# A fused attention, feed-forward and expert kernel: SBUF tiles on the right side moved to multiples of 256 bytes, two operands offset by 32 and 64 bytes

## The chip, the core and the metric

The kernel runs on one core of a Trainium2 chip. Its time is the device time of one execution in microseconds; lower is better. The kernel before takes 744.92 us, the median of three runs (744.52, 744.92 and 745.54).

## What is computed

Three layers follow each other, all in fp32, for 4 sequences of 576 tokens (2304 in all) and a width of 512:

```python
# 1. attention of 8 heads of width 64; heads 0-3 see the last 32 positions, heads 4-7 every fourth of the last 128
attn = softmax(where(mask, q @ k.T / 8, -1e9)) ; x = attn @ v              # -> x [2304, 512]
# 2. feed-forward, squared relu
h = x @ w_in                                  # [512, 2048]
g = s * relu(h) ** 2 + b ; y = g @ w_out      # [2048, 512]
# 3. one of 8 experts per token, chosen by argmax of cosine similarity to an embedding
e = argmax(norm(y) @ norm(emb).T / tau)
out = gate * (relu(y @ w1[e]) @ w2[e])        # 512 -> 1024 -> 512
```

## The kernel before, in words

**Precision.** Each large product is made of three matmuls in the type fp32r: both operands are split into a high and a low part (`xhi`/`xlo`, `wih`/`wil`, `gh`/`gl`, `woh`/`wol`, and for the experts `xh`/`xl`, `wh`/`wl`, `hh`/`hl`), and `mm3` (lines 454 to 458) adds high times high, high times low and low times high into one PSUM bank. Every one of these matmuls has its own weight load: TensorE streams the moving operand of one matmul (`rhs`) while it loads the weights (`lhsT`) of the next, both from SBUF.

**Feed-forward stage** (`main`, `gemm1_mm`, `gemm2`). The tokens are in five groups; groups 0, 2, 3 and 4 have 512 tokens and group 1 has 256. A group takes 16 steps, one per 128 columns of the hidden layer. In each step the first product (`gemm1_mm`) makes 12 matmuls with `wih`/`wil` as weights and x as the moving operand, of 512 columns, or of 256 for group 1. The second product (`gemm2`), two steps later, has `gh`/`gl` as weights and `woh`/`wol` as moving operand, always of 512 columns: 12 matmuls, or 6 for group 1. Hence the first product has 64 steps of 12 matmuls of 512 columns and 16 steps of 12 of 256 columns; the second has 64 steps of 12 and 16 of 6. The attention of the next group, in small matmuls, is put between the steps. ScalarE and VectorE turn the raw weights into high and low parts during the first 22 steps (`Conversion`); after that the weights are resident.

**Where the tiles lie.** SBUF is allocated from both ends. Tiles in pools of the left side start, in the built program, at multiples of 256 bytes wherever a large matmul reads them: `xhi1`/`xlo1` (x of groups 1, 2 and 4, by the table `XH`), `wih`/`wil` of steps 11 to 15, `woh`/`wol` of steps 9 to 15, `gh`/`gl`, and for the experts the weights of odd units (`wp1`) and `hh`/`hl`. Tiles of the right side are laid down below a first tile `edge` (line 632, 8 floats, 32 bytes), and start 192 bytes past a multiple of 256: `xhi0`/`xlo0` (x of groups 0 and 3), `wih`/`wil` of steps 0 to 10, `woh`/`wol` of steps 0 to 8, and the weights of the experts' even units (`wp0`). The experts' x (`xp`, line 1081) lies below small tables and starts 128 bytes past a multiple of 256. Every slice of 128 columns inside these tiles is 512 bytes further, so a whole tile keeps its remainder.

**Expert stage** (`experts`). Tokens are gathered by expert into slots of 128 tokens, and 12 units, each with one expert's weights, always run. A unit serves a pair of slots or a single slot; unit 0 serves two pairs. In a pair, `g1_pair` makes 96 matmuls of 256 columns with the experts' weights as weights and `xh`/`xl` as the moving operand. In a single slot, `g1` has it the other way round: 24 matmuls with `xh`/`xl` as weights and the experts' weights, 512 columns, as moving operand. The second product `g2` makes 24 matmuls of 512 columns per tile, with `hh`/`hl` as weights and the experts' second weights as moving operand. Unit 0 has its weights on the right side and does two pairs; the six units with odd numbers have theirs on the left side and do a pair each; the five even ones behind unit 0 have theirs on the right side and do a single each.

**Order.** TensorE, and in most of the kernel ScalarE and VectorE, run in the order that the program was written in (`manual_schedule`). The change moves no instruction: on all five engines the order is the same, row by row, and so are the waits.

Of the kernel before, what the change touches and what calls it, by code (L numbers as in the profile page):

```python
# [7 lines left out]
F32 = mybir.dt.float32  # L8
F32R = mybir.dt.float32r
# [22 lines left out]
P = 128  # L32
# [4 lines left out]
UT = 256  # L37
NU = NT // UT
G = 512
GU = (2, 1, 2, 2, 2)  # L40
XH = (0, 1, 1, 0, 1)
NG = len(GU)
U0 = [sum(GU[:g]) for g in range(NG + 1)]
GT = [2 * n for n in GU]
T0 = [2 * n for n in U0]
NTE = T0[NG - 1]
SEGS = [(0, 0, 8), (1, 0, 16), (0, 8, 16)] + [(g, 0, 16) for g in range(2, NG)]
ORDER = [(g, f) for g, f0, f1 in SEGS for f in range(f0, f1)]
# [60 lines left out]
class Kern:  # L109
# [176 lines left out]
    def attn_x(self, cs):  # L286
        c, k = cs[0], len(cs)
        un, pr = c["un"], c["pr"]
        g = next(g for g in range(NG) if un < U0[g + 1])
        d0 = UT * (un - U0[g])  # L290
        hi, lo = (x[XH[g]][:, pr:pr + k, d0:d0 + UT] for x in (self.xhi, self.xlo))
        src = c["po"][:, :k * UT].rearrange("c (u t) -> c u t", u=k)
        if c["dil"]:
            src = src.rearrange("c u (j p) -> c u p j", j=4)
            hi, lo = (x.rearrange("c u (p j) -> c u p j", j=4) for x in (hi, lo))
        return hi, lo, src
# [86 lines left out]
    def attn_steps(self, n0, n1, ps):  # L383
# [4 lines left out]
        for n in range(n0, n1, 2):  # L388
            g = next(g for g in range(NG) if n // 4 < U0[g + 1])
            start, period, turn = TEMPO[g - 1]  # L390
# [68 lines left out]

    def gemm1_mm(self, g, fc, kcs=range(4)):  # L460
        n = P * GT[g]
        xh, xl = (x[XH[g]][:, :, :n] for x in (self.xhi, self.xlo))
        if 0 in kcs:
            self.ph = self.psf(f"ph{g}_{fc}")[:, :n]
        for kc in kcs:
            self.mm3(self.ph, self.wih[fc][:, kc], self.wil[fc][:, kc], xh[:, kc], xl[:, kc], kc == 0, kc == 3)
# [55 lines left out]
    def y_norm(self, g):  # L522
        if g < NG - 1:
            self.bg += self.logits_dve(g)
            return
        self.late_ssq = self.lpool.tile([P, 4], F32, tag="ssq", name=f"ssq{g}", bufs=2)
        for i in range(GT[g]):
            junk = self.mpool.tile([P, DM], BF16, tag="gh", name=f"junk{g}_{i}")
            self.nc.scalar.activation(junk, self.ysb[T0[g] + i], AF.Square, accum_out=self.late_ssq[:, i:i + 1])
# [98 lines left out]
    def run(self):  # L628
        tc, nc = self.tc, self.nc
        with tc.tile_pool(name="al", bufs=1, side="right") as al, tc.tile_pool(name="c", bufs=1) as c, \  # L630
                tc.tile_pool(name="dr", bufs=1, space=DRAM) as dr:
            al.tile([P, 8], F32, name="edge")
            self.lpool = c
            self.ydram = dr.tile([NT, DM], F32, name="ydram")
            first, late = ExitStack(), ExitStack()
            right = dict(bufs=1, side="right")
            with tc.tile_pool(name="wl", bufs=1) as wl:
                wr = first.enter_context(tc.tile_pool(name="wr", **right))
                self.weights_setup(wl, wr)
                ac = first.enter_context(tc.tile_pool(name="ac", **right))  # L640
                self.apool = first.enter_context(tc.tile_pool(name="ap", bufs=2, side="right"))
                self.mask = {}
                self.first_masks(ac)
                self.consts(c)
                self.mask_pool = ac

                def late_pools():
                    for nm in ("wp0", "rawp", "rpool", "xp"):
                        setattr(self, nm, late.enter_context(tc.tile_pool(name=nm, reuse_waits="tile", **right)))
                    self.psT = late.enter_context(tc.tile_pool(name="psT", space=PSUM, reuse_waits="tile", **right))  # L650
                self.phase1(wl, first, late, late_pools)
            kw = dict(bufs=1, reuse_waits="tile")
            with tc.tile_pool(name="wp1", **kw) as self.wp1, tc.tile_pool(name="hp", **kw) as self.hp, \
                    tc.tile_pool(name="pad", **kw) as self.pad, tc.tile_pool(name="psE", space=PSUM, **kw) as self.psE:
                self.experts()
            late.close()
# [421 lines left out]
    def xt(self, js, xs):  # L1078

        nc, w = self.nc, P * len(js)  # L1080
        xh = self.xp.tile([P, 4, w], F32R, tag="xh", name=f"xh{js[0]}")
        xl = self.xp.tile([P, 4, w], F32R, tag="xl", name=f"xl{js[0]}")
        for n, (j, x) in enumerate(zip(js, xs)):
            if n and j >= NEARLY:
                px = self.psE.tile([P, 512], F32, tag="h", name=f"px{j}", bufs=3)
            else:
                px = self.bank(f"px{j}", n == 0 and j >= 2)
            for i in range(4):
                nc.tensor.transpose(px[:, P * i:P * i + P], x[:, P * i:P * i + P], self.ident)
            p3 = px.rearrange("p (k t) -> p k t", k=4)  # L1090
            h, l = (y[:, :, P * n:P * n + P] for y in (xh, xl))
            nc.scalar.copy(h, p3)
            self.last_xl = nc.vector.tensor_sub(l, p3, h.bitcast(F32))
        return xh, xl
# [91 lines left out]
    def experts(self):  # L1186
# [63 lines left out]
        with tc.issue_after(self.last_gidx.ins):  # L1250
            self.gates_late()
        self.g2(2, 0, *hts, w[0])
        xt(1)
        behind.append((self.last_xl,))
        for a in range(2):
# [25 lines left out]
        with tc.manual_schedule(engines={mybir.EngineType.Activation, mybir.EngineType.DVE}):  # L1281
            for u in range(1, nstat, 2):
                more = u + 1 < nstat
                hts, part = self.g1_pair(runs[u], *xts.pop(u), w[u])
                h = hook({0: (u, 7), 1: (u, 8), 2: (u + 1, 1), 4: (u + 1, 2), 5: (u + 1, 3), 7: (u + 1, 4)})
                for i in range(4):
                    part(i, h)
                    if more and i == 0:
                        gather(u + 2)
                if more:  # L1290
                    xt(u + 1)
                self.g2(runs[u][0], 0, *hts, w[u], hook({2: (u + 1, 5), 6: (u + 1, 6)}))
                if more:
                    hs = self.g1(runs[u + 1][0], *xts.pop(u + 1), w[u + 1], hook({0: (u + 1, 7), 1: (u + 1, 8)}))
                self.g2(runs[u][1], 1, *hts, w[u], hook({2: (u + 2, 1), 6: (u + 2, 2)}))
                if more:
                    if u + 3 < nstat:
                        gather(u + 3)
                    hts = self.ht(runs[u + 1][0], hs)
                    xt(u + 2)  # L1300
                    self.g2(runs[u + 1][0], 0, *hts, w[u + 1],
                            hook({1: (u + 2, 3), 3: (u + 2, 4), 5: (u + 2, 5), 7: (u + 2, 6)}))
# [68 lines left out]
```

## Time and profile before

| | |
|---|---|
| median of three runs | 744.92 us |
| the profiled execution's own time | 742.73 us |
| its span, first to last instruction | 740.9 us |
| TensorE busy (matmuls) | 725.5 us, 98% of the span |
| VectorE busy | 532.8 us, 72% |
| ScalarE busy | 381.9 us, 52% |
| granted TensorE clock, mean | 0.998 of full speed |

Matmuls are pipelined: one shows as busy for longer than it holds the engine, so the busy time says only that TensorE is hardly ever without work. What a matmul costs is the distance from its start to the start of the next one, which the timeline gives. The shares of ScalarE and VectorE are averages over stages that differ, and a table by stretch is needed to see where one of them is close to full.

### The profile page before, as it was taken

The numbers are of one execution on the slowest core, as the hardware profiler recorded it, in microseconds if no ns is written. First come the engines' busy times: TensorE is split into PE (matmuls) and PEld (weight loads), VectorE is DVE, ScalarE is ACT, GpSimd is POOL, SyncE is SP. The second block draws the span as 40 slices with busy tenths as digits, with TensorE's granted clock in tenths as the row PEclk, the third lists the DMA queues.
The fourth block names the chain that finished last, engine by engine and source line by source line (L and its number), as shares of the span: only waits on it lengthen the run. The fifth ranks groups of instructions, "written<-read, shape, count | busy, mean of one in ns | idle before, by whom it ended". The sixth has DMA issues, their size and how long they took to land. (4 is left out here: it accounts for less than half of the span.)

```text
span 740.9 us, 13198 instructions
## 1 busy us (share of the span) xinstructions
PE 725.5 (98%) x4769; PEld 605.1 (82%) x4769; DVE 532.8 (72%) x1236; ACT 381.9 (52%) x831; POOL 61.6 (8%) x94
## 2 busy tenths in 40 slices
PE   9899999999999999999999999999999999999996
PEld 6677897787888888888888878788888888989894
DVE  6899998765776645877836779369668686868661
ACT  6899665765634424444424226425146565656550
POOL 6000000000000000000000000204213131311011
PEclk9999999999999999999999999999999999999999
DMA  9656653422311101111001006304263077878600
GB/s 278 201 186 212 189 169 127 148 70 74 93 52 58 52 23 43 51 52 58 23 1 58 0 1 227 114 1 132 83 197 103 30 231 261 297 257 285 224 30 26
DMA packets 34039, 87.34 MB, mean 118 GB/s; under 512 B 4326, under 2 KB 4326, under 8 KB 33840
## 3 DMA queue, kind: packets, MB, share of 16 engines
q1 hardware_dynamic: 30608, 76.22, 31.7%
q0 software_dynamic: 3360, 10.23, 4.2%
q8 instruction: 39, 0.64, 0.4%
q14 instruction: 32, 0.26, 0.1%
HBM read 92.72 MB, written 10.22 MB: 139 GB/s over the span
## 5 line engine op out<-in xcount | busy, mean ns | idle before, releaser
L1068 DVE TENSOR_TENSOR wl<-raw,wh 128x1024 fp32r<-128x1024 f32 x96 | 113.7, 1220 | 29.7 <-ACT wh L1067 29.7
L456 PE MATMUL ph<-xhi,wih 128*128 128x512 f32 (+1 forms) x320 | 119.6, 374 | 1.1 <-ACT wih L103 1.1
L458 PE MATMUL ph<-xhi,wil 128*128 128x512 f32 (+1 forms) x320 | 118.6, 371 | 0.9 <-DVE wil L106 0.8
L457 PE MATMUL ph<-xlo,wih 128*128 128x512 f32 (+1 forms) x320 | 118.5, 370 | 0.4 <-DVE xlo L304 0.4
L456 PE MATMUL py<-woh,gh 128*128 128x512 f32 x288 | 116.1, 403 | 0.0
L457 PE MATMUL py<-wol,gh 128*128 128x512 f32 x288 | 113.5, 394 | 0.5 <-DVE wol L106 0.5
L458 PE MATMUL py<-woh,gl 128*128 128x512 f32 x288 | 113.2, 393 | 0.0
L1067 ACT CAST wh<-raw 128x1024 fp32r<-128x1024 f32 x96 | 96.2, 1054 | 8.7 <-DMA raw<-in_moe_w 8.7
L471 ACT ACTIVATE r<-ph 128x512 f32<-128x512 f32 (+1 forms) x80 | 44.2, 553 | 107.4 <-PE ph L458 107.4
L492 DVE SCALAR_TENSOR_TENSOR gl<-r,sb,gh 128x512 fp32r<-128x512 f32 (+1 forms) x64 | 43.7, 683 | 55.4 <-ACT gh L481 55.2
L754 DVE CUSTOM_DVE_ANT_0 junk<-ysb,enb 128x512 bf16<-128x512 f32 x112 | 76.9, 687 | 1.3
L481 ACT ACTIVATE gh<-r,sb 128x512 fp32r<-128x512 f32 (+1 forms) x64 | 42.8, 668 | 66.9 <-PE py L457 60.3
L456 PE MATMUL ph<-xh,wh 128*128 128x256 f32 x256 | 72.4, 283 | 0.7 <-ACT ysb L510 0.7
L457 PE MATMUL ph<-xl,wh 128*128 128x256 f32 x256 | 71.9, 281 | 0.0
L458 PE MATMUL ph<-xh,wl 128*128 128x256 f32 x256 | 71.8, 281 | 0.0
L456 PEld LDWEIGHTS ph<-xhi,wih 128*128 128x128 f32 x320 | 60.1, 188 | 14.1 <-ACT wih L103 2.2
L458 PEld LDWEIGHTS ph<-xhi,wil 128*128 128x128 f32 x320 | 60.1, 188 | 12.7 <-DVE wil L106 2.0
L457 PEld LDWEIGHTS ph<-xlo,wih 128*128 128x128 f32 x320 | 60.2, 188 | 11.9 <-DVE xlo L304 0.9
L456 PE MATMUL po<-wh,hh 128*128 128x512 f32 x168 | 66.9, 398 | 0.0
L458 PE MATMUL po<-wh,hl 128*128 128x512 f32 x168 | 65.9, 392 | 0.0
L457 PE MATMUL po<-wl,hh 128*128 128x512 f32 x168 | 65.9, 392 | 0.0
L458 PEld LDWEIGHTS py<-woh,gl 128*128 128x128 f32 x288 | 54.1, 188 | 12.5
(304 smaller groups left out, 1251.5 us busy)
## 6 DMA issues: line engine op xcount, KB each, us to landing
raw<-in_moe_w SPq DMA_DIRECT2D x96, 512.0 KB
raw<-in_moe_w_in SPq DMA_DIRECT2D x16, 512.0 KB
raw<-in_moe_w_out SPq DMA_DIRECT2D x16, 512.0 KB
v<-in_vw SPq DMA_DIRECT2D x32, 192.0 KB
qk<-in_qkd SPq DMA_DIRECT2D x18, 320.0 KB
ydram<-ysb SPq DMA_DIRECT2D x18, 256.0 KB
qk<-in_qkp SPq DMA_DIRECT2D x15, 272.0 KB
enb<-in_moe_expert_emb SPq DMA_DIRECT2D x1, 2048.0 KB
```

The source lines that it names most:

```text
L456: nc.tensor.matmul(out, lhsT=ah, rhs=bh, start=first, stop=False)
L457: nc.tensor.matmul(out, lhsT=ah, rhs=bl, start=False, stop=False)
L458: nc.tensor.matmul(out, lhsT=al, rhs=bh, start=False, stop=last)
L471: nc.scalar.activation(r, ph, AF.Relu)
L481: nc.scalar.activation(gh, r, AF.Identity, bias=self.sb[:, 1:2])
L492: nc.vector.scalar_tensor_tensor(out=gl, in0=r, scalar=self.sb[:, 1:2], in1=gh.bitcast(F32), op0=ALU.add, op1=ALU.subtract)
L754: ins = nc.vector.tensor_tensor_reduce(out=self.junk, in0=y, in1=self.enb[:, e], scale=1.0, scalar=0.0, op0=ALU.mult, op1=ALU.add, accum_o ...
L1067: nc.scalar.copy(h, r)
L1068: nc.vector.tensor_sub(l, r, h.bitcast(F32))
```

## The change

Three places change. The first tile of the right side grows from 32 to 224 bytes, so all other tiles of that side move down by 192 bytes; those that large matmuls read now start at multiples of 256, but the experts' x, which starts 192 bytes past one (128 before). Group 1's x begins 8 floats (32 bytes) into its tile `xhi1`/`xlo1`. In the experts' single slots x begins 16 floats (64 bytes) into its tile, which puts it at a multiple of 256; in the pairs it stays at the tile's start. Sizes, values and the number of instructions stay as they were.

```diff
 XH = (0, 1, 1, 0, 1)
+XC = (0, 8, 0, 0, 0)
...
-        d0 = UT * (un - U0[g])
+        d0 = XC[g] + UT * (un - U0[g])
         hi, lo = (x[XH[g]][:, pr:pr + k, d0:d0 + UT] for x in (self.xhi, self.xlo))
...
         n = P * GT[g]
-        xh, xl = (x[XH[g]][:, :, :n] for x in (self.xhi, self.xlo))
+        xh, xl = (x[XH[g]][:, :, XC[g]:XC[g] + n] for x in (self.xhi, self.xlo))
...
-            al.tile([P, 8], F32, name="edge")
+            al.tile([P, 56], F32, name="edge")
...
-        xh = self.xp.tile([P, 4, w], F32R, tag="xh", name=f"xh{js[0]}")
-        xl = self.xp.tile([P, 4, w], F32R, tag="xl", name=f"xl{js[0]}")
+        o = 0 if len(js) == 2 else 16
+        xh, xl = (self.xp.tile([P, 4 * w + o], F32R, tag=t, name=f"{t}{js[0]}")[:, o:].rearrange("p (k t) -> p k t", k=4)
+                  for t in ("xh", "xl"))
```

The remainders of the operands of the large matmuls, in bytes past a multiple of 256, before and after:

| product | weights, moving operand before | after |
|---|---|---|
| first product, groups 0 and 3, steps 0-10 | 192, 192 | 0, 0 |
| first product, groups 0 and 3, steps 11-15 | 0, 192 | 0, 0 |
| first product, groups 2 and 4, steps 0-10 | 192, 0 | 0, 0 |
| first product, groups 2 and 4, steps 11-15 | 0, 0 | 0, 0 |
| first product, group 1 (256 columns), steps 0-10 / 11-15 | 192, 0 / 0, 0 | 0, 32 |
| second product, steps 0-8 / 9-15 | 0, 192 / 0, 0 | 0, 0 |
| experts, pairs (256 columns), unit 0 / odd units | 192, 128 / 0, 128 | 0, 192 |
| experts, singles, first product | 128, 192 | 0, 0 |
| experts, second product, units 0 and even / odd | 0, 192 / 0, 0 | 0, 0 |

## Rows read from the trace of the kernel before

**Rows 1.** The page, first two parts: engines' busy time, TensorE's granted clock by slices.

```profile
PE 725.5 (98%) x4769; PEld 605.1 (82%) x4769; DVE 532.8 (72%) x1236; ACT 381.9 (52%) x831; POOL 61.6 (8%) x94
...
PEclk9999999999999999999999999999999999999999
```

**Rows 2.** Waits of TensorE, whole span: waited for, us in total, times, longest us.

```profile
PE ph L456 <- ACT wih L103: 1.1, 1, 1.1
```

**Rows 3.** Busy time by stretch: length, busy us of PE, PEld, DVE, ACT, POOL, clock, DMA.

```profile
28.00:75.00 47.00, 46.16 (x312) 35.85 (x312) 45.37 (x102) 42.74 (x99) 0.19 (x1) 1.00 0.62 204
75.00:125.00 50.00, 48.30 (x301) 42.88 (x301) 47.20 (x95) 30.98 (x63) 0.00 (x0) 1.00 0.46 148
```

**Rows 4.** Groups by line, shapes apart: the second product and one attention group.

```profile
L456 PE MATMUL py<-woh,gh 128*128 128x512 f32 x288 | 116.1, 403 | 0.0
...
L283 PE MATMUL po<-sT,v 96*64 96x64 f32 x512 | 18.9, 225 | 0.9 <-ACT sT L273 0.9
```

**Rows 5.** TensorE's timeline (start us, us, what), group 2, all at 0: 48 matmuls.

```profile
271.15 0.39 PE L456 MATMUL ph<-xhi,wih 128*128 128x512 f32 x1
...
282.03 0.39 PE L456 MATMUL ph<-xhi,wih 128*128 128x512 f32 x1
```

**Rows 6.** Timeline, group 4: starts of three steps of 12 matmuls, steps 5, 3, 6.

```profile
410.37 0.40 PE L456 MATMUL ph<-xhi,wih 128*128 128x512 f32 x1
...
413.16 0.39 PE L456 MATMUL py<-woh,gh 128*128 128x512 f32 x1
...
415.96 0.40 PE L456 MATMUL ph<-xhi,wih 128*128 128x512 f32 x1
```

**Rows 7.** Timeline, group 3: first product, x and weights on the right, step 1.

```profile
287.53 0.39 PE L456 MATMUL ph<-xhi,wih 128*128 128x512 f32 x1
...
290.26 0.39 PE L456 MATMUL py<-woh,gh 128*128 128x512 f32 x1
```

**Rows 8.** Timeline, group 4, first product, step 1.

```profile
388.19 0.39 PE L456 MATMUL ph<-xhi,wih 128*128 128x512 f32 x1
...
390.94 0.39 PE L456 MATMUL py<-woh,gh 128*128 128x512 f32 x1
```

**Rows 9.** Timeline, experts: unit 0's second product; a single's first; unit 1's second.

```profile
520.46 0.39 PE L456 MATMUL po<-wh,hh 128*128 128x512 f32 x1
...
526.05 0.27 PE L1089 MATMUL px<-ident,x 128*128 128x128 f32 x1
...
553.23 0.39 PE L456 MATMUL ph<-wh,xh 128*128 128x512 f32 x1
...
555.99 0.40 PE L456 MATMUL po<-wh,hh 128*128 128x512 f32 x1
...
561.45 0.27 PE L1139 MATMUL pt<-ident,h 128*128 128x128 f32 x1
```

**Rows 10.** Timeline, experts' pairs of 256 columns: first pair, second pair, unit 1.

```profile
479.73 0.28 PE L457 MATMUL ph<-xl,wh 128*128 128x256 f32 x1
...
482.32 0.28 PE L458 MATMUL ph<-xh,wl 128*128 128x256 f32 x1
...
512.30 0.28 PE L456 MATMUL ph<-xh,wh 128*128 128x256 f32 x1
...
515.02 0.28 PE L456 MATMUL ph<-xh,wh 128*128 128x256 f32 x1
...
533.18 0.28 PE L456 MATMUL ph<-xh,wh 128*128 128x256 f32 x1
...
536.02 0.28 PE L456 MATMUL ph<-xh,wh 128*128 128x256 f32 x1
```

**Rows 11.** Timeline, group 1, step 12 and the second product behind it (6 matmuls).

```profile
111.61 0.28 PE L456 MATMUL ph<-xhi,wih 128*128 128x256 f32 x1
...
113.05 0.40 PE L456 MATMUL py<-woh,gh 128*128 128x512 f32 x1
...
114.43 0.28 PE L456 MATMUL ph<-xhi,wih 128*128 128x256 f32 x1
```

## The prediction

> **What bounds the kernel now.** I read the page first, then TensorE's waits, then a table by stretch, then the timeline. The page shows TensorE busy for 98% of the span, the granted clock in the top tenth (nine) in all 40 slices, and VectorE at 72% [rows 1]. So TensorE is the candidate, and it stands at its upper level, 2.4 GHz: nothing is to be had from the clock. In the list of its waits, the longest for a large matmul sums to 1.1 us over the whole span [rows 2]. The table by stretch qualifies this: from 28 to 125 us VectorE is busy for 45.37 of 47 and 47.20 of 50 us [rows 3], because it still converts weights. There a faster TensorE would only wait for VectorE. Behind 125 us TensorE alone sets the pace, and a nanosecond off each matmul is a nanosecond off the end.
>
> So the question is what one matmul costs, from start to start. At 512 columns the timeline gives different prices for the same shape, the same operation and no recorded wait. With both operands on the left side, remainders 0 and 0, 48 matmuls take 282.03 - 271.15 = 10.88 us, **226.7 ns** each [rows 5]. With both on the right side, 192 and 192, 12 take 290.26 - 287.53 = 2.73 us, 227.5 ns [rows 7]. With one on each side, 12 take 413.16 - 410.37 = 2.79 us (moving 0, weights 192) and 415.96 - 413.16 = 2.80 us (moving 192, weights 0): 232.5 and **233.3 ns** [rows 6]. All four combinations of the sides are there. Neither side is slow by itself; what costs is that the remainders differ. TensorE streams one operand while it loads the next matmul's weights, and the two reads get in each other's way by about 6.6 ns per matmul when their places differ by 192 bytes modulo 256.
>
> **The change, term by term.** It adds no instruction, transfer or wait. It only makes remainders equal in every product of 512 columns, and makes a new difference in those of 256. I count behind 125 us alone, by the code's loops.
>
> 1. Second product, steps 0 to 8, right-side moving operand. Of group 0 only step 8 lies behind 125 us (12 matmuls), of groups 2, 3 and 4 all nine steps: 12 + 3 x 9 x 12 = 336. They fall from 233.3 to 226.7 ns [rows 5, 6]: 336 x 6.6 = 2.2 us. (The group has 288 x 3 = 864 in all [rows 4]; the rest are in phase already or in the converting stretch.)
> 2. First product of groups 0 and 3, steps 11 to 15: 2 x 5 x 12 = 120, crossed the same way. At 6.6 ns: 0.8 us.
> 3. First product of groups 2 and 4, steps 0 to 10: 2 x 11 x 12 = 264. Here the rows vary, from 2.75 / 12 = 229.2 ns [rows 8] to 232.5 [rows 6]. The middle, 230.9, less 226.7: 4.2 ns, or 1.1 us.
> 4. Experts' second product with right-side weights: unit 0 has four tiles and five singles one each, 9 x 24 = 216. One tile takes 526.05 - 520.46 = 5.59 us, 232.9 ns; an in-phase tile of unit 1 takes 561.45 - 555.99 = 5.46 us, 227.5 ns [rows 9]. 216 x 5.4 = 1.2 us.
> 5. Experts' singles, first product: 5 x 24 = 120, now 128 against 192, 2.76 / 12 = 230.0 ns [rows 9], then 0 against 0. 120 x 3.3 = 0.4 us.
> 6. Experts' pairs, 256 columns. Units with odd numbers have 0 for the weights and 128 for x: 24 matmuls take 2.84 us, 118.3 ns. The second pair of unit 0, weights 192 and x 128, takes 2.72 us, **113.3 ns** [rows 10]. The change gives all pairs weights 0 and x 192: the same difference, weights 64 bytes past x modulo 256, as unit 0 has today. 6 x 96 = 576 matmuls by 5.0 ns: 2.9 us. This is the term that I trust least: the very first pair has that difference as well, and 22 steps of its timeline (479.73 to 482.32) give 117.7 ns [rows 10]. The spacing therefore has more than one steady rhythm, and which one is taken depends on what ran before. The first pair is broken up at every part by the routing's small matmuls (`experts` calls `wide` and `dots` between its parts); unit 0's second pair and those of the odd units run their parts without such breaks, so I take 113.3. Bounds: 113.3 and 117.7, or 2.9 and 0.3 us.
> 7. Group 1 (192 matmuls of 256 columns, x at 32 past weights at 0) has a difference that no row shows. The nearest rows have 113.3 to 120 ns [rows 10, 11]; step 12 now takes 1.44 us, 120 ns [rows 11]. The bounds by these rows: 192 x 6.7 = 1.3 us gained (120 to 113.3), and, if the steps 0 to 10 stand at 117.7 now and all go to 120, 192 x 2.3 = 0.4 us lost. But these steps lie in the stretch where VectorE has 47.20 of 50 us [rows 3]: VectorE is late next, the gain turns into waits on its low parts, and I take nothing. The same holds for all large matmuls before 125 us.
> 8. Attention and the transposes. Their small matmuls (512 in the largest group [rows 4]) also read right-side tiles that move. No pair of rows compares two remainders of them. I take nothing, and bound it by the 3% that 6.6 ns are of 226.7, on the largest group's 18.9 us busy [rows 4]: 0.6 us either way.
>
> Sum: 2.2 + 0.8 + 1.1 + 1.2 + 0.4 + 2.9 = 8.6 us. ScalarE and VectorE give it no cover to lose behind 125 us; TensorE waits for neither there for a microsecond in any one place. The profiled execution has 742.73 us (span 740.9 and 1.8 around it); it would have 734.1. The median of the runs is 2.2 us above it, so the forecast against the median is 744.9 - 8.6 = **736.3 us**.
>
> The Trainium skill speaks against this sum. "SBUF — State Buffer", section "Who interferes with whom", gives TensorE two read ports, one for the moving operand and one for the weight load, independent of each other, and says that TensorE never waits on anyone. By that rule the place of a tile costs nothing and the change would leave 744.9. The trace disagrees, with 226.7 against 233.3 ns [rows 5, 6].
>
> **The rivals.**
> - *Pairs keep the slow rhythm* (117.7 ns, as the first pair [rows 10]). Then term 6 is 576 x 0.6 = 0.3 us and the sum 6.0: 738.9 us. For it: the one stretch without a restart near it is the only fast one. Against it: once reached, 113.3 holds for three parts of a pair without relapse.
> - *Places don't matter*, and the rows' differences come from the stage: other work on SBUF beside the steps. Then nothing changes: 744.9. The rule of "SBUF — State Buffer" in the Trainium skill, above, would have it so. Against it: group 4 alternates between 232.5 and 233.3 and, in the same group and stage, 226.7 follows once both operands are on the left; and the right side in phase is as fast as the left [rows 5 to 7].
> - *Equal remainders settle in a slow rhythm*, the one that ends slower. In group 1 equal remainders of 0 and 0 do not give 226.7: six matmuls take 1.38 us, 230.0 ns, and those of 256 columns 120 [rows 11]. If all 512-column matmuls took a rhythm above what they have now, the change would lose. The worst that the rows show for any remainders is 233.3. Of these, some 1980 lie behind 125 us; the 1056 of terms 1 to 5 average 232.2 and the rest some 227.5, so the mean now is (1056 x 232.2 + 924 x 227.5) / 1980 = 230.0. At 233.3 the change would add 3.3 x 1980 = 6.5 us, 751.4 us; it decides as soon as the mean passes 230.0 and the pairs gain nothing. Against it: four steps in a row at 226.7 in group 2 [rows 5].
>
> **How the numbers follow.** Forecast 0.50; slow pairs 0.36; places don't matter 0.08; slow rhythm 0.06. A measurement of this kernel can tell about 0.2%, 1.5 us, from no change: faster 0.86, same 0.08, slower 0.06. The range starts at the forecast less the bounds of terms 7 and 8 and half of what the converting stretch could give (276 matmuls of 512 columns by 6 ns, 1.6 us): 736.3 - 1.3 - 0.6 - 0.8, about 733.5. It reaches over the slow pairs with term 8 against us, 738.9 + 0.6, to 739.6. That holds the first two cases.
>
> **What would show it.** In the profile after: steps of 12 at 2.72 us wherever 2.80 stood, in groups 2 to 4; tiles of the experts' second product at 5.46 instead of 5.59 us; the pairs at 2.72 us per part (right) or 2.83 (first rival); TensorE's waits before 125 us longer by about what its matmuls there lose. The prediction is wrong if the crossed steps still take 2.80 us, or if steps take 2.72 and the end does not come earlier: then another engine had been as late as TensorE behind 125 us.

## The result, and the profile after

The changed kernel takes **736.50 us** (median of four runs, 735.18 to 737.65) against 745.09 for the kernel before on the same chip: a ratio of 0.9888, with a 95% interval of 0.9872 to 0.9903, or 8.6 us less. The profiled execution took 737.65 us with a span of 735.9 us; it was the longest of the four. The first part of its page, with each engine's busy time:

```profile
PE 718.5 (98%) x4769; PEld 604.0 (82%) x4769; DVE 533.1 (72%) x1236; ACT 381.9 (52%) x831; POOL 60.9 (8%) x94
```

The counts are those of [rows 1], and so are VectorE's and ScalarE's times to 0.3 us; only TensorE has become shorter, by 7.0 us. `mm3` now stands one line lower (457 to 459). The table by stretch, with the columns of [rows 3]:

```profile
28.00:75.00 47.00, 45.64 (x311) 35.59 (x310) 45.09 (x101) 42.53 (x99) 0.20 (x1) 1.00 0.61 201
75.00:125.00 50.00, 48.30 (x303) 43.08 (x302) 47.73 (x96) 31.38 (x65) 0.00 (x0) 1.00 0.49 149
```

VectorE (third busy time) is as full as before: 45.09 of 47 and 47.73 of 50 us, after 45.37 and 47.20. This stretch has nothing to give. The place to look at is behind 125 us. TensorE's timeline there (start us, us, engine, line, operation), first group 3's step 1 and group 4's three steps of [rows 7] and [rows 6]:

```profile
285.52 0.39 PE L457 MATMUL ph<-xhi,wih 128*128 128x512 f32 x1
...
288.24 0.39 PE L457 MATMUL py<-woh,gh 128*128 128x512 f32 x1
...
406.70 0.39 PE L457 MATMUL ph<-xhi,wih 128*128 128x512 f32 x1
...
409.42 0.39 PE L457 MATMUL py<-woh,gh 128*128 128x512 f32 x1
...
412.14 0.39 PE L457 MATMUL ph<-xhi,wih 128*128 128x512 f32 x1
```

All three steps take 2.72 us, 226.7 ns per matmul, where [rows 6] had 2.79 and 2.80. The experts in the same view: unit 0's second pair, unit 0's second product, unit 1's pair, a single's first product and unit 1's second product, which answer to [rows 9] and [rows 10]:

```profile
507.46 0.28 PE L457 MATMUL ph<-xh,wh 128*128 128x256 f32 x1
...
510.18 0.28 PE L457 MATMUL ph<-xh,wh 128*128 128x256 f32 x1
...
517.56 0.39 PE L457 MATMUL po<-wh,hh 128*128 128x512 f32 x1
...
523.02 0.27 PE L1091 MATMUL px<-ident,x 128*128 128x128 f32 x1
...
530.03 0.28 PE L457 MATMUL ph<-xh,wh 128*128 128x256 f32 x1
...
532.85 0.28 PE L457 MATMUL ph<-xh,wh 128*128 128x256 f32 x1
...
549.95 0.39 PE L457 MATMUL ph<-wh,xh 128*128 128x512 f32 x1
...
552.67 0.39 PE L457 MATMUL po<-wh,hh 128*128 128x512 f32 x1
...
558.11 0.27 PE L1141 MATMUL pt<-ident,h 128*128 128x128 f32 x1
```

Unit 0's second product tile went from 5.59 to 5.46 us, the single's first product from 2.76 to 2.72. But the pair of unit 1 takes 532.85 - 530.03 = 2.82 us (117.5 ns; over all 24 parts of the odd units 2.827, or 117.8) where the prediction had 2.72. Unit 0's second pair still has 2.72, with the same difference between its operands.

**Where the time came from.** The span shrank by only 5.0 us, less than the median did. The profiled execution contains a stop that no other profile of this study has. The timeline of TensorE and ScalarE around it (the bracket is the idle time before, and what ended it):

```profile
512.75 0.37 PE L457 MATMUL ph<-xh,wh 128*128 128x256 f32 x1 [0.37 <-issue]
514.16 0.38 PE L458 MATMUL ph<-xl,wh 128*128 128x256 f32 x1 [1.03 <-issue]
514.29 0.60 ACT L1115 ACTIVATE hh<-ph 128x512 fp32r<-128x512 f32 x1 [2.19 <-remote]
```

Two matmuls that follow each other start 1.41 us apart instead of 0.11, and nothing that the profile shows was waited for. The part of the pair with the stop takes 4.66 us, those beside it 2.72: 1.94 us were lost here. What caused it stays open. So the two kernels are compared further down by a second profile of the changed one.

### The profile page after: what moved, and what is told of

Same layout as the page of the kernel before. It is cut to its first block, busy times and chain, and to the rows that moved or that the text cites. A ratio compares the mean times of both kernels' runs of the same rounds, so it can differ in the third digit from the quotient of the medians.

```text
span 735.9 us, 13198 instructions
## 1 busy us (share of the span) xinstructions
PE 718.5 (98%) x4769; PEld 604.0 (82%) x4769; DVE 533.1 (72%) x1236; ACT 381.9 (52%) x831; POOL 60.9 (8%) x94
## 5 line engine op out<-in xcount | busy, mean ns | idle before, releaser
L459 PE MATMUL ph<-xhi,wil 128*128 128x512 f32 (+1 forms) x320 | 117.8, 368 | 0.9 <-DVE wil L107 0.8
```

The source lines that it names most:

```text
L459: nc.tensor.matmul(out, lhsT=al, rhs=bh, start=False, stop=last)
```

## Experiments

Each expectation names the theories that it weighs, and theories B and C are others in other runs. Theory A is the one behind the prediction: a matmul is dearer when its two operands don't lie at the same remainder modulo 256 bytes. In its sharper form every unequal pair of remainders costs about the same.

### The changed kernel again

No edit. 

> The changed kernel once more, for the rhythm of the experts' pairs and the spread between executions. Theory A (a layout fixes the rhythm): the parts of the six pairs of odd units take 2.83 us again (117.8 ns per matmul), as in the first profile, and the time is 736.5 within 1.5 us. Theory B (the rhythm is taken by chance in each execution): some parts take 2.72 us (113.3 ns), and the runs spread by up to 2.6 us (576 matmuls by 4.5 ns).

Measured: 736.61 us (735.90 to 738.18, five runs), ratio 0.9908 (0.9892 to 0.9925); the profile has a span of 734.3 us and no stop at 512 us. Two starts of TensorE's timeline in the kernel before, group 1's second product behind its last step and the experts' first matmul:

```profile
123.74 0.40 PE L456 MATMUL py<-woh,gh 128*128 128x512 f32 x1
...
479.50 0.38 PE L456 MATMUL ph<-xh,wh 128*128 128x256 f32 x1 [0.68 <-ACT ysb L510]
```

The same two in this run:

```profile
123.76 0.40 PE L457 MATMUL py<-woh,gh 128*128 128x512 f32 x1
...
475.37 0.39 PE L457 MATMUL ph<-xh,wh 128*128 128x256 f32 x1 [0.68 <-ACT ysb L511]
```

In this profile nothing was gained up to 123.7 us. The feed-forward stage behind it went from 479.50 - 123.74 = 355.76 to 351.61 us: **4.15 us**. From the experts' first matmul to the end of the span it went from 740.9 - 479.50 = 261.4 to 258.9 us: **2.5 us**. The other two profiles of the changed kernel have 351.65 and 351.67 us for the first of these, and reach group 1's product at 123.39 and 123.05 us; the second profile of the kernel before reaches it at 125.48. So up to there executions of one kernel differ by 0.7 us and more, and a small gain couldn't be told. All six pairs of the odd units took 117.8 ns again and unit 0's second pair 113.3 again: in this kernel these pairs keep their rhythms from one execution to the next.

### One part of the change at a time

Only the first tile of the right side, without the two offsets:

```diff
-            al.tile([P, 8], F32, name="edge")
+            al.tile([P, 56], F32, name="edge")
```

> Only the first tile of the right side grows; group 1's x and the singles' x are not offset. Theory A (unequal remainders modulo 256 cost some 6 ns per matmul of 512 columns): all crossed steps go to 226.7 ns, only the singles' first product keeps 230 (120 x 3.3 = 0.4 us), so 737 us, 0.4 above the full change. Rival (the offsets carry a part of their own): 739 us or more.

Measured: 736.98 us (736.91 to 737.52), ratio 0.9908 (0.9895 to 0.9922). The singles' first product, whose weights x now stood 192 bytes past the moving operand, took 228.9 ns. This one line gives all but some 0.4 us of the change, and 0.4 is less than the two intervals can tell apart. Unit 0's second pair took 117.8 ns here, as the starts of its second and third part show:

```profile
508.19 0.28 PE L456 MATMUL ph<-xh,wh 128*128 128x256 f32 x1
...
511.01 0.28 PE L456 MATMUL ph<-xh,wh 128*128 128x256 f32 x1
```

In the change it took 113.3, in all three profiles, and neither of the two offsets that are missing here touches this pair, the second product ahead of it or the 18 small matmuls between the two. The offsets alone (next run) do the same against the kernel before: 117.8 after 113.3, at unchanged places. So for this pair neither its own places nor those of the product ahead decide. What does stays open.

Only the two offsets, with the right side left at 192:

```diff
-            al.tile([P, 56], F32, name="edge")
+            al.tile([P, 8], F32, name="edge")
```

> Only the two offsets, with the right side where it was. The singles' x then stands at 192 like their moving operand; group 1's x at 32 against weights at 192 and 0. Theory A: the singles' first product falls to 226.7 ns and gains 0.4 us, group 1 lies in the stretch that VectorE sets, so 744.6 us, the same as before within the noise. Rival (the offsets carry a part): under 743 us.

Measured: 744.09 us (743.50 to 745.04, eleven runs), ratio 1.000 (0.9991 to 1.001). TensorE's timeline, the three steps of group 4 as in [rows 6], then a single's first product:

```profile
411.85 0.40 PE L457 MATMUL ph<-xhi,wih 128*128 128x512 f32 x1
...
414.65 0.39 PE L457 MATMUL py<-woh,gh 128*128 128x512 f32 x1
...
417.45 0.40 PE L457 MATMUL ph<-xhi,wih 128*128 128x512 f32 x1
...
555.04 0.39 PE L457 MATMUL ph<-wh,xh 128*128 128x512 f32 x1
...
557.75 0.39 PE L457 MATMUL po<-wh,hh 128*128 128x512 f32 x1
```

The crossed steps kept their 2.80 us. The single's first product, with both operands at 192, took 2.71 us by these rounded starts (226.7 ns per matmul): equal remainders are enough, they need not be 0. By itself that is too little to be seen in the time.

### The difference, or multiples of 256

All tiles of both sides 64 bytes further than in the changed kernel (edited):

```diff
+            c.tile([P, 16], F32, name="left_edge")
...
-            al.tile([P, 56], F32, name="edge")
+            al.tile([P, 40], F32, name="edge")
```

> The changed kernel with all tiles of both sides moved by 64 bytes: all remainders 64 past where the change puts them, and no difference between two operands is other than in the change. Theory A (the difference counts): 736.5 us, 226.7 ns per matmul. Rival (multiples of 256 themselves count): the 512-column matmuls rise to 230 or 233 ns, and the time to 742 to 745 us.

Measured: 735.49 us (735.33 to 736.08, four runs), ratio 0.9885 (0.9870 to 0.9900). The three steps of group 4:

```profile
407.16 0.39 PE L457 MATMUL ph<-xhi,wih 128*128 128x512 f32 x1
...
409.88 0.39 PE L457 MATMUL py<-woh,gh 128*128 128x512 f32 x1
...
412.60 0.39 PE L457 MATMUL ph<-xhi,wih 128*128 128x512 f32 x1
```

2.72 us each, and no tile that they read begins at a multiple of 256. **The difference counts, not the place.** The counterpart, the kernel before with the right side at 128 instead of 192 and the left at 0:

```diff
-            al.tile([P, 8], F32, name="edge")
+            al.tile([P, 24], F32, name="edge")
```

> The kernel before with the right side moved by 64 bytes only: its tiles stand at 128, the left ones at 0, the experts' x at 64. Theory A: crossed steps cost as much as at 192 (about 233 ns), 745 us; Theory C (the distance counts): another price, between 226.7 and 236 ns per crossed matmul, by 1056 of them 738 to 748 us.

Measured: 743.31 us (742.20 to 745.00, ten runs), ratio 0.9992 (0.9983 to 1.0002). The same three steps start at 411.15, 413.95 and 416.75: 2.80 us each, 233.3 ns. Another difference, the same price; moving the side alone gains nothing.

### What each difference costs

The experts' hidden values `hh`/`hl` are the weights of the second product, and their place can be chosen unit by unit. The first try (changed kernel, edited; the keys are a unit's first slot, the values bytes):

```diff
+HO = {4: 32, 6: 192, 7: 64, 9: 16, 10: 96, 12: 48, 13: 128, 15: 8, 16: 160, 18: 4, 19: 224}
...
-        return [self.hp.tile([P, 8, P * len(js)], F32R, tag=t, name=f"{t}{js[0]}") for t in ("hh", "hl")]
+        w, o = P * len(js), HO.get(js[0], 0) // 4
+        return [self.hp.tile([P, 8 * w + o], F32R, tag=t, name=f"{t}{js[0]}")[:, o:].rearrange("p (k t) -> p k t", k=8)
+                for t in ("hh", "hl")]
```

> The changed kernel with the experts' hidden activations (the weights of the second product, moving operand at 0) at another remainder in each unit: pairs at 32, 64, 96, 128, 160, 224, singles at 192, 16, 48, 8, 4. One look gives a curve of the time of a 512-column matmul over the difference. Theory A (any difference modulo 256 costs about the same): 226.7 ns at no remainder but 0, 233 at all of them. Theory C (reads meet in banks of 64 bytes): 4, 8, 16 and 48 cost little, 64, 128 and 192 cost 5 to 7 ns. In all 300 matmuls by 0 to 6.6 ns: 736.5 to 738.5 us.

Measured: 736.54 us, one run (before: 744.26). As a curve it failed. The tiles share two buffers that grew by the largest offset, 224 bytes, so `hl` lay 32 bytes away from `hh`, and each product mixed two differences: all took 231 to 236 ns, unit 0's too, which was meant as the control. It showed something else: the pairs of slots 4, 7, 10 and 19, whose own operands were untouched, took 113.3 ns, those of 13 and 16 took 117.8.

The same was tried with x of the pairs:

```diff
+XO = {0: 192, 2: 224, 4: 32, 7: 64, 10: 96, 13: 128, 16: 160, 19: 0}
...
-        o = 0 if len(js) == 2 else 16
+        o = XO.get(js[0], 64) // 4
```

> The changed kernel with the pairs' x at another remainder in each unit: 128 and 160 in unit 0, then 224, 0, 32, 64, 96, 192 in units 1, 3, 5, 7, 9, 11, against weights at 0. Theory A (the difference sets the rhythm of 256-column matmuls): 128 gives 118.7 ns and 0 gives 120 as in the profile before, 192 gives 117.8, and some remainder gives 113.3 steadily. Theory B (the rhythm is what the matmuls before leave behind): the remainders between 192 and 224 give no order, and no part holds 113.3.

Measured: 739.00 us, one run. It failed in the same way: the larger buffers moved both bases, `xl` lay 32 bytes below `xh`, the singles' x was no longer in phase (231.1 ns), and every pair took 117.6 to 118.9 ns.

Both were repeated with tiles that grow by a whole 256 bytes, so that the bases stay where they are. For `hh`/`hl`, with the same table `HO`:

```diff
+        w, o = P * len(js), HO.get(js[0], 0) // 4
+        return [self.hp.tile([P, 8 * w + 64], F32R, tag=t, name=f"{t}{js[0]}")[:, o:o + 8 * w].rearrange("p (k t) -> p k t", k=8)
+                for t in ("hh", "hl")]
```

> As the first curve of the hidden activations, but both tiles (high and low) grow by 256 bytes, so that high and low stand at the same remainder: pairs at 32, 64, 96, 128, 160, 224, singles at 192, 16, 48, 8, 4, unit 0 at 0, all against a moving operand at 0. In the first curve the growth of 224 bytes had put the low part 32 bytes off the high part. Theory A (any difference costs): 226.7 ns in unit 0, 231 to 234 at every other remainder, the few bytes of 4, 8 and 16 included. Theory C (banks of 64 bytes): 4, 8, 16 and 48 stay below 229. The pairs of 256 columns, unchanged here, tell a second thing: if what runs before them sets their rhythm, some of the six go to 113.3 ns although their own operands stand as in the change; if their own places set it, all six stay at 117.8.

Measured: 737.13 us, one run (before: 744.35). TensorE's timeline: a pair behind the second product at 192 bytes, a second product tile at 64, one at 16 with its second matmul, and a pair behind that:

```profile
566.66 0.28 PE L458 MATMUL ph<-xh,wh 128*128 128x256 f32 x1
...
569.38 0.28 PE L458 MATMUL ph<-xh,wh 128*128 128x256 f32 x1
...
586.34 0.40 PE L458 MATMUL po<-wh,hh 128*128 128x512 f32 x1
...
591.95 0.27 PE L1144 MATMUL pt<-ident,h 128*128 128x128 f32 x1
...
593.61 0.47 PE L458 MATMUL po<-wh,hh 128*128 128x512 f32 x1
...
593.92 0.39 PE L459 MATMUL po<-wl,hh 128*128 128x512 f32 x1
...
599.14 0.28 PE L458 MATMUL ph<-xh,wh 128*128 128x256 f32 x1
...
601.96 0.28 PE L458 MATMUL ph<-xh,wh 128*128 128x256 f32 x1
...
604.79 0.28 PE L458 MATMUL ph<-xh,wh 128*128 128x256 f32 x1
```

At 64 bytes 24 matmuls take 591.95 - 586.34 = 5.61 us, 233.8 ns by these rounded starts (233.3 in mid-stream). At 16 bytes the first start is 0.31 us ahead of the second (a single's first gap, in every kernel), and the other 23 take 599.14 - 593.92 = 5.22 us, 227.0 ns. The whole curve, in mid-stream, for 512 columns and weights that lie so many bytes past the moving operand, modulo 256 (each value is that of one or two tiles in one profile, good to some 0.4 ns; the value at 0 is also that of the whole feed-forward stage):

| bytes | 0 | 4 | 8 | 16 | 32 | 48 | 64 | 96 | 128 | 160 | 192 | 224 |
|---|---|---|---|---|---|---|---|---|---|---|---|---|
| ns | 226.7 | 232.5 | 230.6 | 226.7 | 233.2 | 233.2 | 233.3 | 234.3 | 232.4 | 233.5 | 228.9 | 233.2 |

Theory A holds for 0 and for nine of the others; 16 costs nothing and 192 costs a third. A theory in which only a larger unit of 64 bytes counts falls with 4 and 8. The pairs behind 192 (2.72 us) and behind 8 took 113.3 ns, the other four 117.8, as the last two rows show (2.83 us). Their own operands were the same in all six: **the rhythm of these six pairs goes with the product that TensorE does just before them**, with nothing between. But the tiles that the pairs write had been moved too, so this is not yet shown.

The pairs, with x at various places and the weights at 0:

```diff
+XO = {0: 192, 2: 224, 4: 32, 7: 64, 10: 96, 13: 128, 16: 160, 19: 16}
...
+        o = XO.get(js[0], 64) // 4
+        xh, xl = (self.xp.tile([P, 4 * w + 64], F32R, tag=t, name=f"{t}{js[0]}")[:, o:o + 4 * w].rearrange("p (k t) -> p k t", k=4)
```

> As the first curve of the pairs' x, but with tiles that grow by 256 bytes, so that x's high and low part stand at the same remainder and the singles where the change puts them. Pairs' x at 128 and 160 (unit 0), 224, 0, 32, 64, 96 and 208 (units 1, 3, 5, 7, 9, 11), weights at 0. If places set the rhythm of the 256-column matmuls, 128 gives 118.7 ns and 0 gives 119 to 120 as in the profile before, and one of the others may hold 113.3; if what runs before sets it, the six pairs, which all follow a second product at 226.7, all lie at 117 to 120 with no order over the remainder. Time 736 to 738 us.

Measured: 738.95 us, one run (before: 744.35). The offsets add to the tile's own 192 bytes. Apart from the first (at 128), which the routing breaks up, each pair held one value to its last part:

| x past the weights, bytes | 0 | 32 | 64 | 96 | 128 | 160 | 208 | 224 |
|---|---|---|---|---|---|---|---|---|
| ns, 256 columns | 120.0 | 116.7 | 117.8 | 120.0 | 118.6 | 117.3 | 119.2 | 118.3 |

At 256 columns equal remainders are among the dearest, and 113.3 was seen at 192 alone.

### Using it

If the product ahead sets the rhythm, putting the second product ahead of each pair at 192 bytes should give 113.3 in all six, at the small price of that difference (changed kernel, with the tiles of the clean curve):

```diff
+HO = {2: 192, 6: 192, 9: 192, 12: 192, 15: 192, 18: 192}
```

> The change, with the hidden activations of the five singles and of unit 0's second pair 192 bytes further, so that the second product ahead of each of the six pairs runs out of phase. In the clean curve the pair behind a single at 192 ran at 113.3 ns. If what runs before sets the pairs' rhythm, all six pairs go from 117.8 to 113.3 ns and gain 576 x 4.5 = 2.6 us, less about 7 x 24 x 2.2 ns = 0.4 us in the products moved: 734.4 us against the change's 736.6 in the same comparison. If that one pair was chance, some or none of the six go over, and the time is 736.6 to 737.

Measured: **733.75 us** (732.96 to 735.40, four runs), ratio 0.9865 (0.9850 to 0.9880). Beside it on the same chip, the changed kernel as it is:

> The changed kernel beside it, on the same chip: 736.6 us within 1 us, pairs of odd units at 117.8 ns as in its two profiles so far. If the rhythm were taken by chance in each execution, another pattern would show here.

Measured: 735.82 us (735.68 to 736.93, five runs), ratio 0.9902 (0.9889 to 0.9916). The first pair behind a single in the version with 192:

```profile
567.57 0.28 PE L458 MATMUL ph<-xh,wh 128*128 128x256 f32 x1
...
570.29 0.28 PE L458 MATMUL ph<-xh,wh 128*128 128x256 f32 x1
```

All six pairs take 2.72 us per part, 113.3 ns, and the tiles that they write stand at 0 as in the change: modulo 256 only the products ahead differ, so they decide for these six. Worked out beforehand: 576 x 4.5 = 2.6 us gained, 7 tiles x 24 x 2.2 = 0.4 paid, 2.2 net; measured 735.82 - 733.75 = 2.1. In the two profiles the pairs gained 2.4 us and the products ahead of them paid 0.2. This version is faster than both kernels.

### The kernel before again

No edit. 

> The kernel before once more, for a second profile: its first profile took 742.73 us, 2.2 to 2.8 below its timed runs. If the crossed steps have more than one rhythm, some steps take another time per matmul than in the first profile; if it was a stall that came and went, the steps are the same and a few gaps of 1 to 2 us differ.

Measured: 744.86 us, span 743.2, against 742.73 and 740.9 of the profile that the prediction worked from. Every product has the prices of the first profile but for 12 matmuls of the first pair, which took 113.2 ns instead of 117.8: in that pair the rhythm is not the same in every execution. Group 0's step 6 starts 0.8 us later in the converting stretch, and this is the table by stretch behind it:

```profile
120.00:123.50 3.50, 1.80 (x8) 1.05 (x7) 3.26 (x7) 2.19 (x5) 0.00 (x0) 1.00 0.01 5
123.50:126.90 3.40, 3.40 (x14) 3.11 (x15) 1.74 (x4) 0.89 (x2) 0.00 (x0) 0.50 0.00 0
```

The same two stretches in the first profile:

```profile
120.00:123.50 3.50, 1.79 (x13) 1.36 (x11) 3.47 (x7) 1.31 (x3) 0.00 (x0) 1.00 0.02 5
123.50:126.90 3.40, 3.40 (x18) 2.86 (x17) 2.51 (x9) 1.40 (x3) 0.00 (x0) 1.00 0.26 72
```

TensorE was busy for 1.80 of 3.50 us, while it stood behind the last converted weights, and then had a granted clock of 0.50, its lower level of 1.2 GHz. In the first profile it stood there as long, busy for 1.79 of 3.50 us, and kept 1.00; these runs don't show what makes the difference. The timeline of the second profile in that stretch:

```profile
125.91 0.63 PE L457 MATMUL py<-wol,gh 128*128 128x512 f32 x1
126.33 0.63 PE L458 MATMUL py<-woh,gl 128*128 128x512 f32 x1
126.76 0.47 PE L456 MATMUL py<-woh,gh 128*128 128x512 f32 x1
```

The starts lie 0.42 to 0.43 us apart. So 3.41 us hold the work of about half as much, and some 1.6 us are lost. The first profile of before has none of this.

## Why the prediction was right, and where it was not

The forecast was 736.3 us and the time is 736.5, inside the range. But the sum of 8.6 us did not come about as written: two of its steps were off, in opposite directions.

- *What bounds the kernel*: right. Behind 125 us the end moved by what TensorE's matmuls lost, and no other engine became late.
- *Terms 1 to 3* (second product, first product of groups 0, 3, 2 and 4): predicted 2.2 + 0.8 + 1.1 = 4.1 us, measured 4.15 in the feed-forward stage. But that the two agree so closely is in part chance. Added up step by step, from a step's first start to the start of what follows it, the three terms gained 1.75 + 0.70 + 1.03 = 3.5 us; the other 0.7 came from products that the sum took as "in phase already", 0.28 of it from the first products of groups 0 and 3, steps 0 to 10, and 0.35 from the second product of steps 9 to 15. Some of these were dearer beside crossed products: group 3's step 9, with 192 and 192, runs from 338.78 to 341.52 us in the kernel before, 2.74 us, and takes 2.72 in the changed one. The mechanism is shown from both sides: the edge alone gives it, the offsets alone don't, another place with equal remainders does, another difference doesn't.
- *Terms 4 and 5* (right-side weights of the experts' second product; singles' first product): predicted 1.2 and 0.4. The sums of the second product's tiles fell by 0.38 us in unit 0 and 0.63 in the singles, so 1.0; the singles' first product by 0.37. Right.
- *Term 6* (pairs of the odd units) **failed**: "24 matmuls take 2.84 us, 118.3 ns ... The change gives all pairs ... the same difference ... as unit 0 has today", hence 576 x 5.0 = 2.9 us. They went from 118.7 to 117.8: 0.5 us. That the difference of a pair's own operands decides its rhythm was wrong. At that difference both 113.3 and 117.8 are steady, and for these six pairs the product ahead chooses; that was shown with the operands untouched, and then used. For unit 0's second pair, the row from which 113.3 was taken, it is not the whole reason: with the edge alone it had 117.8 behind the same product. The sentence in term 6 that "which one is taken depends on what ran before" was right, the reason drawn from it (breaks by small matmuls) was not: parts of the odd units run without such breaks and stay at 117.8, while the first three stretches of the first pair, breaks and all, ran at 113.3 to 113.4 in the changed kernel. It is the first rival's mechanism that took place. Its price was 0.3 us for the term, and 0.5 was measured.
- Not in the sum: unit 0's two pairs together became 0.27 us shorter and the second product of the odd units, whose places did not change, 0.22. So the experts gave 0.38 + 0.63 + 0.37 + 0.50 + 0.27 + 0.22 = 2.4 us of the 2.5 found, where 4.5 were forecast.
- *Term 7* (group 1, and all before 125 us): right within the spread. Group 1's steps have 1.40 us per 12 matmuls instead of 1.41, and the second product behind its last step starts at 123.76, 123.39 and 123.05 us in the three profiles of the change, after 123.74 and 125.48 in those of before. The sign that was to go with it, longer waits of TensorE there, can't be told from the spread: the waits for the first product's converted weights between 28 and 124 us sum to 1.1 and 2.2 us in the two profiles of before, and to 1.6, 1.6 and 1.1 in those of the change.
- *Term 8* (small matmuls): no effect is left over that would need it.
- *From the profiled execution to the median*: the prediction carried over 2.2 us that lay between the two. Undisturbed profiles differ by 740.9 - 734.3 = 6.6 us, not 8.6. But the changed kernel's median lies only 736.61 - 736.03 = 0.6 us above such a profile. The missing 2.0 us of the sum and these 1.6 cancelled by luck. Had the two not met, the first rival's 738.9 would have been nearer.

The rival in which places don't matter falls. By the Trainium skill ("SBUF — State Buffer", section "Who interferes with whom"), TensorE's two read ports are independent of each other and it waits on nobody. The runs disagree: 226.7 against 233.3 ns, by nothing but an address. What is shown is that the price follows the difference of the addresses; that the two reads meet in SBUF is an explanation that no run here tests. The rival in which equal remainders settle in a slow rhythm falls for 512 columns and would have held for 256, at 120.0 ns; the change gives no operands of 256 columns equal remainders.

**Open.** The medians gained 8.6, 7.3 and 7.8 us in three comparisons, where profiles without a stop gained 6.6 and 6.9. The half-clock stretch was in five of the fourteen profiles, among them one of before, and in none of the three of the change as it is; both the version with offsets alone and the one with 192 had it. The mean granted clock of whole executions tells more: it is 0.995 or 0.996 in the five profiles with the stretch and 0.997 to 0.999 in the nine without. By that mark 2 of the 14 executions of the change had it, at 737.98 and 738.18 us its two longest, and 13 of 40 of the kernel before. These are too few to say that the change makes it rarer. Nor is it all that lay between the first profile and the median: executions of before without it, by the same mark, took 742.4 to 744.9 us. And it is open what sets the rhythm of unit 0's two pairs.

## What to carry to other kernels

Where TensorE is the bound and every matmul loads its own weights, compare the start-to-start distance of matmuls of one shape across stages; if it differs, tabulate the operands' addresses modulo 256 before looking for waits, and bring the two to the same remainder: 3% of each 512-column matmul for one line of allocation. Don't carry that rule to another width without measuring: at 256 columns equal remainders are among the dearest. And before a forecast adds the distance between a profiled run and a median, a second profile of the same kernel tells whether it is a property of the kernel or of that execution.

## What the runs showed of the hardware that was not expected

- The price is no smooth function of the distance and not symmetric: 64 bytes cost 6.6 ns of 226.7 and 192 cost 2.2, 16 cost nothing, 8 and 4 cost 3.9 and 5.8. At 192 group 4's first product in the kernel before had 229.2 [rows 8] while the second product beside it was in phase, and 232.5 [rows 6] once that was crossed, too: what runs around a matmul plays a part. Why 16 is free isn't known.
- A stream of 256-column matmuls has two steady rhythms at the same addresses, 113.3 and 117.8 ns. The one that it starts with holds for all four parts of a pair, 96 matmuls and 11 us, and it was the same in all three profiles of the changed kernel. Six pairs took it from the product ahead; a seventh had 113.3 in the change and 117.8 with the edge alone, behind the same product.
- After the same stop of TensorE, busy for 1.80 and 1.79 of 3.50 us, the granted clock fell to 0.50 for 3.41 us in one execution of the kernel before and stayed at 1.00 in another.
